# Gating copies on GpSimd, an expert-major normalisation tile and a new front order in an attention and expert-mixture kernel

## The chip, the cores and the metric

The kernel runs on one core of a Trainium2 chip. The metric is the device time of one execution in microseconds (us); a lower time is better. The time before is 957.84 us, the median of three runs (957.78 to 959.23).

A core has five engines with a queue each. PE (TensorE) multiplies matrices, and its rows in the profile are split into matmuls (PE) and weight loads (PEld). DVE (VectorE), ACT (ScalarE) and POOL (GpSimd) work on elements, and SP (SyncE) only issues transfers here. Each engine works through its own queue in order. Transfers are issued from SP's, POOL's and ACT's queues and are carried out by 16 DMA engines.

## The reference

Linear attention on q, k and v (8 batches, 8 heads, 576 tokens, 64 wide) gives an input x of 4608 tokens by 512. Eight experts with 1024 hidden units work on all tokens. The weights P of the experts come from a gate that is normalised over experts and over tokens, eight times in turn.

```python
def phi(x):
    return np.where(x > 0, x, np.exp(x) - 1.0) + 1.0
q_p, k_p = (phi(q), phi(k))
kv = np.einsum('bhsd,bhse->bhde', k_p, v)
z = np.sum(k_p, axis=2)
num = np.einsum('bhsd,bhde->bhse', q_p, kv)
den = np.einsum('bhsd,bhd->bhs', q_p, z)[..., None] + 1e-06
...
logits = x @ w_gate
P = np.exp(logits - logits.max())
for _ in range(8):
    P /= P.sum(1, keepdims=True) + 1e-09
    P /= P.sum(0, keepdims=True) + 1e-09
    P *= N / E
for e in range(E):
    h = np.maximum(x @ w1[e], 0.0)
    out += P[:, e:e + 1] * (h @ w2[e])
```

## The kernel before

**Tiling.** The 4608 tokens are cut into nine groups of 512. SBUF holds x transposed as xT. The expert products are done in two ways. A plain unit runs the full products: `layer1` (L781) and the second layer (L1081). All other units use a Strassen-like scheme with seven products instead of eight, for both layers: `pair` (matmuls at L896) for the first and `layer2` (L1197) for the second. Each needs combinations of its operands: of x (made on DVE at L826 to L831 and stored in DRAM as the blocks xd), of w1 (tile W, L1123), of w2 (tile T, L1137) and of the hidden units (tile S, L1168).

**Stages.** First comes the front, about 110 us: attention batch by batch (`att`), with units of expert 0 between its steps. Behind it come the rest of expert 0 and the normalisation (`sinkhorn`, about 124 to 177 us), and then experts 1 to 7, of which each has nine units of about 12.15 us.

**x blocks.** From expert 1 on the seven blocks of x are read back from DRAM by `x_load` (L873, queue SP) into ten buffers xs0 to xs9 that are reused in turn. The groups form five sub-blocks: (0), (1,2), (3,4), (5,6) and (7,8). The loads of a sub-block are issued as PE frees buffers. The numbers `n` of `l1_half` count half units: n = 0 is sub-block 0, n = 1 and 2 are sub-block 1, n = 3 and 4 sub-block 2, n = 5 and 6 sub-block 3. The list `first_x` collects loads of x, and the weight loads of expert 2 name it as a dependence.

**Weights.** `load_w1` and `load_w2` (issue at L337, queue POOL) fetch the weights of one expert into one of two buffers each. POOL also carries the input loads of the front (L411), two products in each round of the normalisation (L628 and L640), and one accumulation of an output tile in each half unit (L1238), whose operand st ACT has written into one of two staging tiles (L1235).

**Normalisation.** In each of eight rounds POOL multiplies P0 by the row factor Rr (L640) into wt, DVE sums wt over the tokens for each expert into gs (L644), PE sums over the partitions (L649), DVE inverts (L656, L658), POOL multiplies by the column factor cc (L628), and DVE sums over experts and inverts (L635 to L637).

**Order.** `_Plan` is a list scheduler that runs when the program is built. Each task has an engine, a cost, a latency `lat` and a priority. A task of the kind "dma" stands for a transfer; it emits no instruction, and a dependence on it places the dependent task later in the plan but is not by itself a wait on the chip. The waits on the chip follow from the data that an instruction touches. The string `_FRONT` fixes the order of the first tasks by hand (number and engine letter: p PE, a ACT, d DVE, g POOL, s SP, m dma, n none); behind it the scheduler decides. `_FRONT` reaches as far as the last units of sub-block 2 of expert 1.

Of the kernel before, what the change touches and what calls it, by code (L numbers as in the profile page):

```python
# [141 lines left out]
107n 600n 1n 100n 40s 41m 42s 43m 2p 44g 45m 3p 68g 69m 4p 5p 70g 71m 6p 7p 72g 73m 8p 101g  # L142
102m 9p 10p 47d 46a 0g 11p 12p 103g 104m 48d 13p 52n 53a 14p 141g 142m 54d 15p 105g 106m 16p 55d 17p
18p 19p 20p 49n 139g 140m 56p 50p 57d 21p 51a 22p 75d 74a 114g 115m 23p 24p 58p 25p 26p 59a 76d 27p
143g 144m 80p 62a 64p 60p 81n 82n 85d 28p 83a 29p 65d 30p 86a 77n 112g 113m 31p 32p 84d 61a 78p 87d
33p 79a 34p 63a 35p 116g 117m 66p 88p 67d 36p 89a 37p 108g 109m 38p 39p 92a 94p 90p 601p 91a 95d 110g
111m 602p 93a 96p 151p 97d 603p 153n 152n 154a 604p 605p 607p 155d 606a 609p 166g 167m 156d 611p 613p 608d 145a 168g
169m 146d 615p 614a 612d 98g 99m 124p 616d 617p 125n 126n 127a 147d 195g 196m 148n 618a 149p 128d 619p 150d 118a 170g
171m 119d 157p 637n 158a 120d 197g 198m 159p 129d 121n 122p 160a 123d 161a 610d 164p 130p 623p 193g 194m 131a 165d 620d
162p 132p 621p 133a 163d 134a 135p 222g 223m 622p 136d 624p 629a 224g 225m 173d 625p 631a 172a 137p 178p 138d 626p 179n  # L150
180n 181a 249g 250m 174d 638p 226g 227m 182d 640p 633d 627p 639d 175n 183d 205p 176p 641d 206n 207n 208a 628p 253g 254m
177a 209d 280g 281m 642p 199a 200d 184p 643a 644p 201d 278g 279m 185a 210d 646p 202n 228a 645d 186p 203p 647d 187a 648p
204d 188a 229d 211p 191p 305g 306m 658p 212a 192d 307g 308m 635a 230d 213p 189p 214a 650p 190d 231n 649a 234p 651d 232p
235n 236n 251g 252m 237a 256d 652p 282g 283m 255a 238d 656p 670n 233d 215a 220p 653d 332g 333m 239d 309g 310m 216p 221a
217d 240p 659p 241a 257d 242p 666d 218p 243a 657p 258n 219d 284a 285d 261p 259p 262n 263n 264a 359g 360m 671p 260d 336g
337m 673p 265d 672a 244a 266d 675p 674d 664a 267p 247p 677p 268a 248d 676a 286d 269p 245p 270a 679p 246d 287n 678d 290p
288p 680d 292n 291n 293a 681p 312d 311a 294d 660p 295d 271a 661p 388g 389m 289d 363g 364m 274p 296p 275d 683p 297a 361g
362m 313d 682a 272p 317p 339d 314n 654p 318n 319n 320a 273d 685p 338a 321d 315p 556d 298p 392g 393m 316a 655p 340d 563d
299a 322d 334g 335m 668d 276p 684a 300a 704p 277a 323p 301p 686d 302d 706p 365a 324a 390g 391m 303p 703n 662a 705d 325p
304d 326a 327a 415g 416m 689p 344p 346n 345n 347a 366d 564d 341n 342p 343a 367d 395d 348d 690p 697d 708p 330p 331d 371p  # L160
444g 445m 472g 473m 394a 442g 443m 451s 452s 446g 447m 453s 481s 372n 687p 349d 328p 688p 374a 707a 368n 373n 375d 474g
475m 350p 351a 709a 710p 352p 353a 565d 329d 396d 376d 557d 558d 369p 370a 476g 477m 482s 712p 483s 713d 355p 377p 354a
356d 693p 378a 400p 357p 397n 417g 418m 402n 401n 695d 711d 358d 421a 403a 404d 694p 405d 714p 715d 422d 398p 478a 379p
399a 380a 381a 419g 420m 716p 384p 449d 385d 423d 406p 407a 559s 560m 718p 691p 448a 408p 409a 382p 692p 383d 427p 428n
429n 424n 744n 717a 701d 425p 719d 430a 479d 745p 746a 747p 410a 431d 450d 432d 699a 426a 570d 571d 386p 387a 726p 433p
566s 567m 413p 414d 480d 572d 749p 411p 412d 577d 578d 579d 748a 434a 561s 562m 568s 569m 435p 436a 751p 573s 574m 575s
576m 488p 490n 485n 486p 489n 750a 580s 581m 491a 727p 492d 493d 487a 752a 734a 740d 753p 755p 438p 437a 439d 494p 495a
582s 583m 754a 724p 584d 484g 496p 497a 440p 441d 756a 585d 741d 722p 457p 458n 459n 460a 454n 455p 725p 757p 759p 586d
456d 498a 461d 462d 587s 588m 589s 590m 591g 597n 758a 732a 742d 501p 502d 760a 463p 464a 743d 723p 730a 499p 500d 465p
761d 466a 467a 598g 599m 762d 720p 468p 721p 469d 767p 763d 470p 728a 765p 592n 790n 768a 764d 773p 471d 554n 783d 736d  # L170
784d 785d 786s 787m 1014s 1015m 555p 766a 1016s 1017m 503p 771p 504a 505n 506d 737d 507g 791p 772a 792a 769p 805p 788s 789m
738d 1018s 1019m 1020s 1021m 1022s 1023m 508d 739d 841d 795p 796a 775p 1024s 1025m 1026s 1027m 1056s 1057m 1058s 1059m 776d 806a 797p
509p 510d 798a 793p 842d 794a 811p 812a 511g 801p 802d 799p 807p 808a 770a 815p 512d 809p 803p 804a 810a 513g 813p 816d
817p 843d 814d 800d 514d 777p 849p 818a 778a 819d 863p 864a 515p 516d 517g 899d 900d 820d 518d 774d 848n 865p 866a 823p
901d 519g 869p 870a 824a 871p 872d 867p 868a 873p 874d 520d 851p 821d 829p 850a 855p 856a 830a 852a 853p 825p 844s 845m
854a 521p 522d 523g 859p 826d 860d 524d 525g 833p 827p 861p 822d 857p 858d 862a 875p 526d 593g 594m 595g 596m 834d 907p
831p 527p 957d 528d 876a 921p 923p 922a 529g 832d 877d 878d 530d 531g 879d 835p 836a 906n 924a 909p 927p 925p 928a 926a
883p 929p 930d 881p 908a 913p 532d 533p 958d 959d 960s 961m 828a 914a 931p 884d 932d 882a 910a 911p 534d 535g 917p 918d
880d 885p 887p 888a 912a 915p 536d 919p 891p 933p 920a 934a 889p 1060s 1061m 902s 903m 916d 537g 538d 892d 539p 886d 540d
965p 1006d 541g 967p 968a 893p 542d 543g 979p 890d 935d 966a 894a 981p 971p 904s 905m 972a 964n 939p 940a 846s 847m 975p  # L180
973p 969p 970a 982a 936d 976d 544d 1007d 943p 977p 962s 963m 974d 941p 980a 937d 985p 1008d 545p 983p 986a 987p 1009d 978a
989p 546d 984a 1028p 988d 547g 945p 1029a 990d 942a 938d 1030p 991p 548d 1034p 1031a 947p 946d 1035a 549g 992a 1036p 550d 1032p
1037d 1038p 1033a 949p 1039d 551p 1040p 950d 1042p 552d 1044p 1043a 553d 951p 1045a 948d 1041a 1048p 1005n 1062s 1063m 1050p 1046p 1049a
1052p 995p 1070p 1072p 1051d 1064s 1065m 780d 1066s 1067m 1053d 1068s 1069m 1047a 667d 1152s 1153m 944a 1154s 1155m 952a 1073a 663d 1054p
993p 1156s 1157m 1055a 996p 1071a 1126d 1002d 779d 1076p 1127d 1077a 696a 1078p 1074p 1075a 1080p 1518n 999p 1081d 634d 994p 1010d 1011d
1082p 1012d 636d 1084p 1001d 1086p 1085a 1000p 1087a 1090p 1092p 1091a 1088p 632a 997p 1013d 1083a 1094p 1089a 630d 1079d 1093d 1098p 1004a
998p 1099a 1095d 1100p 1096p 1128d 1101a 1129d 1104p 1106p 1003d 1102p 1105a 1130p 1132p 1133d 1097a 1131a 1135p 1134d 1108p 1140p 1109d 1143p
# [52 lines left out]
def kernel(  # L240
# [375 lines left out]
    def sinkhorn():  # L616
# [9 lines left out]
        for it in range(8):  # L626
# [12 lines left out]
            def f_b(_):  # L639
                nc.gpsimd.tensor_tensor(out=wt, in0=P0_sb,  # L640
                                        in1=Rr[:, :, None].broadcast_to([P, NTT, E]), op=ALU.mult)
# [771 lines left out]
```

## Time and profile before

| | |
|---|---|
| median of three runs | 957.84 us |
| the profiled execution | 960.11 us |
| its span (first to last instruction) | 958.3 us |
| mean granted clock of PE | 0.996 |
| idle time of PE in the span | 17.8 us |
| longest sums of waits of PE | on q loads 3.2 us, on x blocks 3.5 us, on the first memset 1.3 us |
| moved by DMA | 112.75 MB, mean 118 GB/s |

A stretch of the profile lists the busy time of each engine in it, the clock that PE was granted and the share of time in which the DMA engines were busy. A row of a timeline gives start, duration, engine, source line, operation, output and input, and in brackets the idle time just before it and what ended that idle time. "us to landing" is the time from the issue of a transfer to its end. Line numbers (L...) are those of the kernel before; in the changed kernel the lines behind L621 stand one further down, and those behind L1004 five.

### The profile page before, as it was taken

To read this page: it belongs to the slowest core of one execution; us is meant where nothing else is said; L and a number is where in the kernel's file an instruction comes from. 1 tells how busy PE (TensorE), PEld (TensorE's weight loads), DVE (VectorE), ACT (ScalarE), POOL (GpSimd) and SP (SyncE) were. 2 spreads that over 40 slices of the span, in tenths; PEclk is the share of its full clock that TensorE was granted. 3 is DMA by queue.
4 is the path that set the end of the run, shared out by engine and by line. 5 is a ranking of instruction groups with operands and counts; after the bars stand their busy time and mean duration, and the time that the engine had idled before them with its cause. 6 is when DMAs were issued, how large, how long until landed. Compare 5 with 4: busy or idle time off the path is not lost.

```text
span 958.3 us, 19980 instructions
## 1 busy us (share of the span) xinstructions
PE 940.5 (98%) x7856; PEld 636.7 (66%) x7856; DVE 772.2 (81%) x1477; ACT 569.8 (59%) x1015; POOL 156.5 (16%) x220
## 2 busy tenths in 40 slices
PE   8999999989999999999999999999999999999997
PEld 3444488656677666766667666766667666776665
DVE  7789999868887888878888888878887888877776
ACT  6789855656655555555555555555555555555551
POOL 6333013011111111111112111111112111111110
PEclk9999999999999999999999999999999999999999
DMA  9989676263226222652226322542226522215554
GB/s 244 261 196 192 198 166 149 77 147 96 78 79 125 78 77 78 152 115 74 66 76 135 101 78 78 129 98 75 72 73 153 120 78 78 72 45 166 165 133 132
DMA packets 82570, 112.75 MB, mean 118 GB/s; under 512 B 7340, under 2 KB 46764, under 8 KB 82476
## 3 DMA queue, kind: packets, MB, share of 16 engines
q1 hardware_dynamic: 56876, 75.59, 26.0%
q0 software_dynamic: 24848, 34.78, 19.4%
q8 instruction: 61, 1.00, 0.4%
q10 hardware_dynamic: 752, 1.11, 0.3%
q14 instruction: 33, 0.27, 0.1%
HBM read 119.69 MB, written 17.69 MB: 143 GB/s over the span
## 4 chain that ended last, share of the span: by engine, by line
PE 80%; DVE 4%; DMA 1%; issue 0%; POOL 0%; DVEq 0%; POOLq 0%
PE ye L1197 34%; PE hq L896 22%; PE R L896 11%; PE Zye L1197 6%; PE Zye L896 6%; DVE hb L930 1%; DMA xs<-xd 1%; DVE xT L1168 1%; PE ye L1081 1%; PE hq L1293 0%; DVE gs L644 0%; PE R L1293 0%; DVE acc L1215 0%; DVE ut L635 0%; DVE acc L1228 0%
## 5 line engine op out<-in xcount | busy, mean ns | idle before, releaser
L1228 DVE SCALAR_TENSOR_TENSOR acc<-ye,P_sb,acc 128x256 f32<-128x256 f32 x620 | 268.1, 479 | 131.7 <-PE ye L1197 129.1
L1197 PEld LDWEIGHTS <-S 128*128 128x128 f16 x1984 | 194.2, 98 | 46.9 <-DVE S L1168 0.2
L1197 PE MATMUL ye<-T,S 128*128 128x256 f16 x1488 | 193.1, 273 | 0.0
L1238 POOL TENSOR_TENSOR acc<-acc,st 128x256 f32<-128x256 f32 x124 | 88.3, 731 | 636.5 <-ACT st L1235 620.9
L1197 PEld LDWEIGHTS <-hb 128*128 128x128 f16 x1584 | 155.3, 98 | 43.7 <-issue 1.7
L896 PEld LDWEIGHTS <-W 128*128 128x128 f16 x1248 | 122.1, 98 | 88.4 <-DMA xs<-xd 2.5
L927 ACT ACTIVATE hb<-hq 128x512 f16<-128x512 f32 x134 | 80.0, 597 | 137.7 <-PE hq L896 134.7
L896 PE MATMUL R<-xs,W 128*128 128x512 f16 (+1 forms) x560 | 150.1, 358 | 2.0 <-DMA xs<-xd 2.0
L896 PE MATMUL hq<-xs,W 128*128 128x512 f16 (+1 forms) x560 | 150.0, 358 | 0.0
L896 PE MATMUL hq<-xs,w 128*128 128x512 f16 (+1 forms) x560 | 139.8, 358 | 0.1
L896 PEld LDWEIGHTS <-w 128*128 128x128 f16 x936 | 91.7, 98 | 61.3 <-issue 2.4
L924 ACT ACTIVATE hb<-Zye 128x512 f16<-128x512 f32 x134 | 80.1, 597 | 38.9 <-PE Zye L896 38.2
L930 DVE CUSTOM_DVE_ANT_0 hb<-hq,sx 128x512 f16<-128x512 f32 x126 | 86.5, 687 | 15.0 <-PE hq L896 14.8
L1235 ACT ACTIVATE st<-Zye,P_sb 128x256 f32<-128x256 f32 x124 | 52.5, 470 | 75.8 <-PE Zye L1197 74.7
L917 ACT COPY sx<-hq 128x512 f32<-128x512 f32 x126 | 73.5, 583 | 37.6 <-PE hq L896 37.5
L913 ACT COPY Zye<-hq 128x512 f32<-128x512 f32 x134 | 77.9, 581 | 23.6 <-PE hq L896 23.4
L930 DVE CUSTOM_DVE_ANT_0 hb<-R,sx 128x512 f16<-128x512 f32 x126 | 86.3, 685 | 5.7 <-ACT sx L917 4.6
L1168 DVE TENSOR_TENSOR S<-hb 128x1024 f16<-128x1024 f16 x124 | 84.9, 685 | 5.9 <-ACT hb L927 5.9
L896 PE MATMUL Zye<-xs,w 128*128 128x512 f16 (+1 forms) x280 | 75.4, 359 | 1.5 <-DMA xs<-xd 1.5
L921 ACT COPY sx<-R 128x512 f32<-128x512 f32 x126 | 74.4, 591 | 1.4 <-PE R L896 1.4
L1197 PE MATMUL ye<-w,hb 128*128 128x256 f16 x528 | 69.3, 275 | 0.5 <-DVE acc L1228 0.5
L1197 PE MATMUL Zye<-w,hb 128*128 128x256 f16 x528 | 68.4, 273 | 0.0
(125 smaller groups left out, 947.1 us busy)
## 6 DMA issues: line engine op xcount, KB each, us to landing
xs<-xd SPq DMA_DIRECT2D x196, 256.0 KB, 3.4
w<-in_moe_w_dram POOLq DMA_DIRECT2D x17, 512.0 KB, 7.9
kin<-in_k_dram POOLq DMA_DIRECT2D x15, 576.0 KB, 7.3
out_dram<-acc SPq DMA_DIRECT2D x61, 128.0 KB, 2.4
w<-in_moe_w_dram POOLq DMA_DIRECT2D x7, 1024.0 KB, 9.9
xs<-xd SPq DMA_DIRECT2D x49, 128.0 KB, 3.3
vv<-in_v_dram POOLq DMA_DIRECT2D x16, 288.0 KB, 7.7
hb<-in_q_dram POOLq DMA_DIRECT2D x15, 288.0 KB, 7.2
```

The costliest lines, as they stand in the source:

```text
L896: nc.tensor.matmul(dst_[:, p, :] if parts == 2 else dst_.rearrange("p a b -> p (a b)"), lhsT=lhs(p, c), rhs=blk[i](c), start=(first and p ...
L913: nc.scalar.copy(out=Zt[1], in_=gX["tile"])
L917: nc.scalar.copy(out=gs2["tile"], in_=gX["tile"])
L921: nc.scalar.copy(out=gs5["tile"], in_=gR["tile"])
L924: nc.scalar.activation(out=dst(0, 0), in_=Zt[1], func=AF.Relu)
L927: nc.scalar.activation(out=dst(1, 0), in_=gX["tile"], func=AF.Relu)
L930: nc.vector._custom_dve(TENSOR_ADD_SAT, out=out_, in0=ps, in1=sb, s0=3.0e38, s1=0.0)
L1168: nc.vector.tensor_tensor(out=Sx[:, i], in0=a0, in1=a1, op=op)
L1197: nc.tensor.matmul(bank(g_)[:, s, :], lhsT=lhs(s, kk), rhs=rhs(kk), start=(new and s == 0 and kk == 0), stop=(kk == 3), skip_group_check=True)
L1228: nc.vector.scalar_tensor_tensor(out=dst(), in0=bank(g_)[:, s, :], scalar=P_sb[:, gg, e:e + 1], in1=dst(), op0=ALU.mult, op1=ALU.add)
L1235: nc.scalar.mul(out=gst["tile"], in_=bank(g_)[:, s, :], mul=P_sb[:, gg, e:e + 1])
L1238: nc.gpsimd.tensor_tensor(out=dst(), in0=dst(), in1=gst["tile"], op=ALU.add)
```

## The change

There are four edits.

1. *Copies.* `first_x` and `second_x` no longer collect the loads of x themselves. At n = 3 and n = 5 a new POOL instruction copies four elements of the last block of the sub-block into the tile `gate`. The loads of expert 2's w1 depend on the first copy, that of w2 on the second.

```diff
         if q == 0:
             st["x"] = x_load(d, un)
-            if n in (1, 3):
-                (first_x if n == 1 else second_x).extend(t for _, t, _ in st["x"].values())
+            if n in (3, 5):
+                gl, tl_, _ = list(st["x"].values())[-1]
+
+                def f_xg(_, gl=gl):
+                    nc.gpsimd.tensor_copy(out=gate, in_=gl["tile"][:, 0, 0, 0:4])
+                (first_x if n == 3 else second_x).append(add(("pool", 0.15), f_xg, deps=[tl_], use=[gl], prio=un - 400.0))
```

2. *Normalisation.* The product by the row factor is written in expert order, so that the sum over tokens reads neighbouring elements.

```diff
+        wc = wt.rearrange("p g e -> p (g e)").rearrange("p (e g) -> p e g", e=E)
...
-                nc.gpsimd.tensor_tensor(out=wt, in0=P0_sb,
+                nc.gpsimd.tensor_tensor(out=wc.rearrange("p e g -> p g e"), in0=P0_sb,
                                         in1=Rr[:, :, None].broadcast_to([P, NTT, E]), op=ALU.mult)
...
-                nc.vector.tensor_reduce(gs, wt.rearrange("p g e -> p e g"), AXX.X, ALU.add)
+                nc.vector.tensor_reduce(gs, wc, AXX.X, ALU.add)
...
-            a = add(("dve", 1.0), f_r, deps=last, prio=-200.0)
+            a = add(("dve", 1.03), f_r, deps=last, prio=-200.0)
             a = add(("pool", 0.9), f_b, deps=[a], prio=-200.0)
-            a = add(("dve", 0.42), f_g, deps=[a], prio=-200.0)
+            a = add(("dve", 0.46), f_g, deps=[a], prio=-200.0)
```

3. *Costs and latencies in the plan.* A w2 load in one piece counts 5.2 us instead of 2.6, and the input loads of attention get a latency of 2.4 instead of 1.95, but for the first two calls of `att`.

```diff
-            ts_.append(add(("dma", costs[len(ts_)] if costs else 2.6), lambda _: None, deps=[ti],
+            ts_.append(add(("dma", costs[len(ts_)] if costs else 5.2 / len(pieces)), lambda _: None, deps=[ti],
...
-            tin[nm] = fadd(("dma", 1.425), lambda _: None, deps=[ti], use=[gr, *gsw], prio=pr, lat=1.95,
+            tin[nm] = fadd(("dma", 1.425), lambda _: None, deps=[ti], use=[gr, *gsw], prio=pr, lat=1.95 if n < 2 else 2.4,
```

4. *The order.* `_FRONT` is replaced as a whole.

```diff
-107n 600n 1n 100n 40s 41m 42s 43m 2p 44g 45m 3p 68g 69m 4p 5p 70g 71m 6p 7p 72g 73m 8p 101g
...
+1n 600n 100n 107n 40s 41m 42s 43m 2p 3p 0g 4p 44g 45m 5p 6p 68g 69m 7p 8p 70g 71m 9p 72g
...
```

What this moves in the built programs:

- POOL builds the identity (task 0g) before the first input load instead of after the fifth transfer. The third k load of POOL's queue stands ahead of the third q load; before, it stood two loads behind it.
- PE has 24 first-layer matmuls in a row ahead of the transposes (L484) of that third q load; before, it had 20.
- Expert 1's w1 goes out in two steps, after the first and after the fourth round's first product, and w2 after the sixth; before, w2 went first of all and both halves of w1 after the fourth. DVE's combinations of w1 begin after the fifth round instead of after the sixth.
- Of expert 2's weights, w1 now stands behind the first copy and one accumulation, and w2 behind the second copy. Before, w2 and both halves of w1 stood together behind the first accumulation of expert 1.
- From about 195 us of the span of before on, where expert 1's second layer begins with its seven products, the order of PE's matmuls is the same in both programs.

More of the change, by code (lines that the diff above doesn't have):

```diff
@@ L147 @@
[L147 to L151, printed above, removed]
@@ new lines @@
+64p 34p 65d 35p 116g 117m 63a 36p 88p 66p 89a 37p 67d 38p 39p 92a 108g 109m 90p 94p 601p 91a 95d 110g
+111m 602p 93a 151p 96p 153n 152n 603p 154a 97d 604p 605p 155d 607p 606a 609p 156d 168g 169m 611p 613p 608d 166g 167m
+146d 615p 614a 145a 617p 119d 195g 196m 616d 118a 147d 124p 193g 194m 619p 126n 125n 120d 127a 148n 170g 171m 149p 637n
+612a 128d 150a 620d 157p 121n 98g 99m 122p 158a 129d 123a 610d 159p 164p 160a 618d 161a 130p 222g 223m 621p 131a 623p
+165d 162p 132p 163d 133a 622p 197g 198m 134a 624p 629d 137p 226g 227m 631d 178p 625p 179n 180n 181a 138d 627p 173d 172a
@@ new lines @@
+182d 628p 174d 249g 250m 135p 635a 205p 136d 224g 225m 626p 206n 207n 208a 200d 251g 252m 638p 183d 640p 209d 175n 199a
+639d 176p 201d 278g 279m 642p 177a 228a 641d 282g 283m 184p 229d 644p 185a 202n 210d 643a 186p 203p 187a 646p 204d 253g
+254m 188a 645d 305g 306m 191p 211p 648p 212a 192d 647a 230d 189p 213p 656p 214a 190d 231n 649a 256d 234p 232p 236n 235n
+633d 237a 650p 309g 310m 233d 255a 238d 652p 285d 215a 220p 332g 333m 670n 239d 280g 281m 653d 218p 221a 240p 219d 658p
+241a 651d 284a 261p 257d 216p 262n 659p 263n 264a 217d 359g 360m 258n 657p 307g 308m 265d 259p 664a 266d 242p 671p 243a
@@ new lines @@
+260d 286d 244a 267p 247p 660p 268a 248d 661p 311a 666d 269p 312d 245p 673p 270a 287n 246d 290p 674a 672d 288p 292n 291n
+293a 313d 675p 336g 337m 271a 388g 389m 294d 677p 334g 335m 295d 289a 654p 338a 676d 363g 364m 296p 274p 361g 362m 297a
+679p 275d 678a 272p 680d 298p 314n 655p 299a 273d 339d 317p 315p 319n 318n 320a 415g 416m 681p 316d 390g 391m 300a 321d
+683p 322d 682a 276p 668a 340d 685p 366d 277a 684a 556d 303p 703n 323p 704p 324a 304d 563d 344p 705a 301p 345n 444g 445m
+686d 689p 347a 341n 346n 302d 392g 393m 706p 662a 348d 365a 342p 564d 557d 325p 446g 447m 343a 690p 558d 326a 349d 442g
@@ new lines @@
+443m 708p 327a 707d 367d 328p 350p 710p 329d 351a 394a 709d 330p 352p 368n 395d 687p 353a 331d 472g 473m 712p 354a 711d
+371p 396d 369p 372n 373n 474g 475m 374a 697d 451s 714p 476g 477m 452s 421a 453s 375d 693p 370d 713a 400p 355p 401n 417g
+418m 688p 403a 356d 481s 376d 357p 695a 716p 402n 397n 404d 715a 482s 358d 377p 694p 378a 405d 717a 483s 379p 398p 559s
+560m 380a 718p 399d 419g 420m 381a 565d 484g 566s 567m 384p 406p 561s 562m 691p 407a 385d 701a 422d 408p 382p 409a 692p
+383d 568s 569m 410a 719d 427p 744n 413p 423d 428n 429n 745p 430a 414d 747p 746a 431d 478a 424n 425p 570d 386p 479d 426a
@@ new lines @@
+448a 432d 749p 571d 387a 748a 577d 411p 433p 726p 434a 572d 412d 573s 574m 750a 435p 575s 576m 578d 751p 436a 480d 699a
+449d 488p 485n 486p 489n 490n 491a 579d 724p 450d 580s 581m 487a 582s 583m 492d 725p 437a 727p 732a 493d 440p 734a 740d
+494p 753p 495a 441d 752a 741d 496p 438p 497a 720p 454n 439d 498a 742d 457p 499p 743d 459n 458n 721p 460a 500d 755p 754a
+461d 728a 455p 756a 757p 456a 462d 584d 501p 463p 759p 464a 502d 758a 465p 760d 468p 466a 722p 761d 467a 723p 585d 762d
+765p 730a 469d 790n 586d 470p 767p 471d 587s 588m 763d 554n 555p 783d 503p 766a 784d 769p 785d 504a 768a 736d 505n 786s
@@ new lines @@
+543g 941p 972a 939p 979p 964n 970a 980a 975p 976d 981p 940a 982a 973p 544d 974d 985p 945p 987p 943p 986a 977p 946a 978a
+988d 545p 546d 983p 984a 989p 547g 990d 1028p 1030p 1029a 949p 548d 549g 938d 1034p 991p 942a 1031a 947p 1036p 1032p 550d 950d
+948d 1035a 1038p 1039d 951p 551p 1040p 1033a 552d 553d 1037d 1005n 992a 952a 1042p 1043a 993p 994p 1044p 1048p 1041a 696a 1045a 665a
+995p 1049a 1050p 1046p 897a 1052p 1070p 1062s 1063m 1001a 1064s 1065m 1072p 1010d 1047a 1071a 996p 1073a 1011d 1012d 700d 1053d 1054p 1076p
@@ L236 @@
+2143a 2140p 2218d 2298s 2146p 2141a 2299m 2145d 2190p 2300s 2192p 2147d 2191a 2301m 2173p 2219d 2193a 2148p 2220d 2196p 2174d 2149a 2302s 2198p
+2175d 2197a 2303m 2194p 2221d 2222p 2195a 2199d 2224p 2223a 2227p 2225d 2226d 2200p 2228a 2232p 2230a 2201d 2229g 2235p 2231g 2233d 2234d 2202p
+2236d
 """
```

149 lines of the change are left out of this document (61 added, 88 removed).

## The prediction

> **What bounds the kernel now.** I read the page first, then the stretches, then what PE waited for.
>
> ```profile
> span 958.3 us, 19980 instructions
> PE 940.5 (98%) x7856; PEld 636.7 (66%) x7856; DVE 772.2 (81%) x1477; ACT 569.8 (59%) x1015; POOL 156.5 (16%) x220
> PE 80%; DVE 4%; DMA 1%; issue 0%; POOL 0%; DVEq 0%; POOLq 0%
> ```
>
> TensorE (PE) is busy for 940.5 of 958.3 us, and 80% of the chain that ended last is PE work. Both programs send PE the same number of instructions (15690 rows each when the orders are laid side by side, the 38 filler matmuls among them). So the change can move the time only through the 17.8 us in which PE idles and the stretches in which its clock is reduced. In the stretches of the span:
>
> ```profile
> 200.00:220.00 20.00, 16.55 (x101) 10.34 (x100) 13.98 (x29) 10.47 (x20) 3.44 (x5) 0.91 0.91 197
> 300.00:400.00 100.00, 100.00 (x710) 69.17 (x708) 80.58 (x157) 56.31 (x106) 15.06 (x21) 1.00 0.35 91
> ```
>
> The columns are length, then busy time of PE, weight load, DVE, ACT and POOL, then PEclk, DMA share and GB/s. From 300 us on nothing is to be had before the tail: PE is busy for 100 of 100 us at full clock. In 200 to 220 it idles 3.45 us, and the granted clock is 0.91. The timeline of PE shows where:
>
> ```profile
> 201.97 0.59 PE L896 MATMUL R<-xs,W 128*128 128x512 f16 x2
> ...
> 208.00 0.61 PE L896 MATMUL R<-xs,W 128*128 128x512 f16 x2 [1.97 <-DMA xs<-xd]
> 210.08 1.01 PE L896 MATMUL Zye<-xs,w 128*128 128x512 f16 x2 [1.48 <-DMA xs<-xd]
> ...
> 231.57 0.59 PE L896 MATMUL R<-xs,W 128*128 128x512 f16 x2
> ```
>
> Two matmul pairs of expert 1 wait for x blocks (tile xs) of sub-block 2 that are still under way. Two finer stretches give the clock's share, and two early ones will be needed below:
>
> ```profile
> 25.00:30.00 5.00, 3.45 (x66) 1.54 (x59) 4.69 (x8) 4.30 (x6) 1.69 (x3) 0.89 1.24 207
> 30.00:35.00 5.00, 5.00 (x28) 1.64 (x27) 2.56 (x5) 2.85 (x4) 1.92 (x3) 0.77 1.29 262
> ...
> 206.00:211.00 5.00, 1.55 (x6) 0.58 (x6) 2.67 (x5) 0.60 (x2) 0.00 (x0) 0.88 1.12 270
> 211.00:216.00 5.00, 5.00 (x36) 3.87 (x35) 2.03 (x5) 2.66 (x5) 0.52 (x1) 0.78 1.10 263
> ```
>
> The loss in clock is 5 x 0.12 + 5 x 0.22 = 1.7 us. The stall costs 1.97 + 1.48 + 1.7 = 5.15 us.
>
> **Why the blocks are late.** POOL's timeline and the transfers:
>
> ```profile
> 198.74 2.43 POOL L337 DMA_DIRECT2D w<-in_moe_w_dram  x3
> ...
> 215.48 2.27 POOL L1238 TENSOR_TENSOR acc<-acc,st 128x256 f32<-128x256 f32 x3 [14.31 <-ACT st L1235]
> 227.63 0.81 POOL L1238 TENSOR_TENSOR acc<-acc,st 128x256 f32<-128x256 f32 x1 [9.88 <-ACT st L1235]
> 232.81 0.72 POOL L1238 TENSOR_TENSOR acc<-acc,st 128x256 f32<-128x256 f32 x1 [4.38 <-DVE acc L1228]
> 239.78 0.95 POOL L1238 TENSOR_TENSOR acc<-acc,st 128x256 f32<-128x256 f32 x1 [6.25 <-ACT st L1235]
> ```
>
> ```profile
> xs<-xd SPq DMA_DIRECT2D x196, 256.0 KB, 3.4
> w<-in_moe_w_dram POOLq DMA_DIRECT2D x17, 512.0 KB, 7.9
> w<-in_moe_w_dram POOLq DMA_DIRECT2D x7, 1024.0 KB, 9.9
> ...
> xs<-xd SPq DMA_DIRECT2D x10, 256.0 KB, 11.7
> w<-in_moe_w_dram POOLq DMA_DIRECT2D x2, 512.0 KB, 17.1
> ```
>
> All three loads of expert 2's weights leave POOL from 198.74 on, just when SP sends the x blocks whose buffers PE frees about 200. A block lands in 3.4 us over the whole run, and in 11.7 us in the stretch from 180 to 230. The DMA engines are full there (share 1.12 and 1.10). In the program of before nothing holds the weights back behind the blocks.
>
> **The change part by part.**
>
> *The copies (-5.15).* In the changed program w1 of expert 2 stands behind a POOL copy that reads the last x block of sub-block 2 and waits for its transfer; one accumulation on POOL stands between. The load of w2 stands behind a copy that reads the last block of sub-block 3. So the blocks of sub-block 2 have the engines to themselves. The buffer of the block that stalled first comes free about 1.5 us before the pair at 201.97 (the pairs run through the blocks in one order), and 200.5 + 3.4 lands two microseconds ahead of its need at 206.03 (208.00 - 1.97). I take the whole 5.15 off. The bounds are 0 and 5.15.
>
> What is paid: two copies, each like this one, on an engine that is busy for 16% of the span.
>
> ```profile
> L445 POOL CAST gate<-vv x1: 292/292/292, 95.0 to 95.0; 128x4 f32<-128x4 f16 x1
> ```
>
> Behind the first copy wait one accumulation and w1. Its block is freed by the pair at 201.97 and lands about 206.3; the accumulation after it could not run before 215.48 - 5.15 = 210.3 anyway. So w1 leaves at 211.1, and its second half 0.75 us later, landing near 220 by the 7.9 us row. DVE needs it next:
>
> ```profile
> 154.85 0.20 DVE L658 RECIPROCAL cc<-Dc 128x8 f32<-128x8 f32 x1
> 160.49 0.65 DVE L1123 TENSOR_TENSOR W<-w 128x1024 f16<-128x1024 f16 x1
> ...
> 229.55 0.68 DVE L1123 TENSOR_TENSOR W<-w 128x1024 f16<-128x1024 f16 x1
> 258.40 0.94 DVE L1137 TENSOR_TENSOR T<-w 128x1024 f16<-128x1024 f16 x1
> ```
>
> The weight combination keeps its place in DVE's order, so it comes at 229.55 - 5.15 = 224.4, four microseconds after w1. If that cover went, DVE would stop with all evictions behind it. The second copy waits for a block that the pair at 231.57 - 5.15 = 226.4 frees; it lands near 230.5. POOL stands from 223.3 until then. Behind it queue w2 (leaves at 231, lands at 241, needed at 253) and the accumulation that ran at 232.81, now at 231.7 instead of 227.7. ACT has two staging tiles: the next one (accumulated at 239.78 - 5.15 = 234.6) is free already. ACT would be held only if the copy lasted until about 239. Cost: nothing.
>
> *The front's order (-1.7).* With the latency of later loads entered as 2.4 instead of 1.95, PE meets its loads 0.45 us later relative to their issue. Four waits in the attention part are of this kind:
>
> ```profile
> 56.90 0.48 PE L484 MATMUL att<-ident,hb 64*64 64x64 f16 x36 [0.82 <-DMA hb<-in_q_dram]
> ...
> 78.48 0.48 PE L484 MATMUL att<-ident,hb 64*64 64x64 f16 x36 [1.30 <-DMA hb<-in_q_dram]
> 96.39 0.48 PE L484 MATMUL att<-ident,hb 64*64 64x64 f16 x36 [0.35 <-DMA hb<-in_q_dram]
> 97.97 0.70 PE L454 MATMUL kv_ps<-vv,t 64*64 64x128 f16 x36 [1.10 <-DMA vv<-in_v_dram]
> ```
>
> 0.45 + 0.45 + 0.35 + 0.45 = 1.7 us off; at most all 3.57. The loss bound is another wait of the same kind at each place, +3.6. In the first 40 us four more matmuls stand ahead of the transposes of POOL's third q load, but a k load is now ahead of that q in POOL's queue, and the identity is built before the first load. These pull both ways: I take 0, between -3.25 (25 to 35 us: 1.55 us of idle and 0.55 + 1.15 of clock) and +3.25, the same loss once more.
>
> *Normalisation (0).* The scaled terms are written in expert order, and the sum over tokens then reads contiguously.
>
> ```profile
> L644 DVE TENSOR_REDUCE gs<-wt x8: 656/668/675, 126.5 to 173.2; 128x8 f32<-128x288 f32 x8
> L640 POOL TENSOR_TENSOR wt<-P_sb,Rr x8: 682/685/936, 125.1 to 172.5; 128x288 f32<-128x288 f32 x8
> L635 DVE TENSOR_REDUCE ut<-wt x7: 439/446/453, 130.4 to 171.2; 128x36 f32<-128x288 f32 x7
> ```
>
> ```profile
> PE R L649 <- DVE gs L644: 0.9, 2, 0.4
> ```
>
> The reduce should go from 0.668 to the 0.446 of its contiguous sister, 8 x 0.22 = 1.8 us of DVE; PE waited 0.9 us for it in all, and that is the most to gain. No row has a POOL write with a stride. I bound it between nothing and the slowest row of the same line, 0.936, so +0.25 x 8 = 2.0 us, against the 1.8 won: 0, from -0.9 to +0.2.
>
> [...]
>
> *Sum.* -5.15 - 1.7 + 0 + 0 = -6.85 us. The profiled execution took 960.11 us, 1.8 around its span; it becomes 953.3. The median of the runs, 2.27 below it, becomes 957.84 - 6.85 = **951.0 us**.
>
> **The rivals.**
>
> (a) *The front gives everything:* all 3.57 and 3.25 go, and the gs waits too: 957.84 - 5.15 - 3.57 - 3.25 - 0.9 = 945.0; half of that beyond the forecast is about 948. For it: all these are load waits. Against: DMA share 1.24 and 1.29 says that early loads wait for bandwidth, which no order makes.
>
> (b) *Part of the stall stays,* since the late blocks still share the engines with earlier ones: 1.48 us without loss of clock, 952.5. [...]
>
> (c) *The copies do not hold the weights,* or the blocks are late for another cause: only the front's 1.7 comes, 956.1. Against: the copy waits for the transfer's semaphore in the built program.
>
> (d) *Slower: expert 1's w1 comes too late.* Its second half still leaves after the fourth scaling,
>
> ```profile
> 145.40 1.48 POOL L337 DMA_DIRECT2D w<-in_moe_w_dram  x2
> ```
>
> ```profile
> w<-in_moe_w_dram POOLq DMA_DIRECT2D x1, 512.0 KB, 5.4
> ```
>
> ```profile
> 150.00:155.00 5.00, 4.58 (x42) 3.89 (x41) 4.86 (x13) 3.22 (x7) 0.94 (x1) 1.00 0.71 143
> ```
>
> but DVE's combination is now one iteration earlier, behind the cc at 154.85 instead of at 160.49. It has 9.6 us instead of 15. At 17.1, the slow row of its kind, DVE stops 7.5 us, and there, busy for 4.86 of 5 us, it can absorb nothing: evictions, scaling and the buffers that open after normalisation all follow. With one loss of clock and a repeat at the x blocks behind it (1.7 + 1.97): 951.0 + 7.5 + 3.7 = 962. It decides from a landing of 9.6 us, and makes the kernel slower from about 13. Against: 5.4 us at this place.
>
> (e) *The front loses at every place:* 957.84 - 5.15 + 3.6 + 3.25 = 959.5, or about 957.5 at two thirds.
>
> **How the numbers follow.** Forecast with (b): 0.68, own range 948.5 to 954.5. (a) 0.12, (c) 0.05, (d) 0.07, (e) 0.08. The range is 946.5 to 957.0: it cuts off (d), most of (e) and the far end of (a). A measurement of this kernel tells 0.2%, 1.9 us, from no change. Faster (below 955.9): forecast and (b), (a), and half of (c), 0.83; within 0.2%: 0.06; slower: (d) and part of (e), 0.11.
>
> **What would show it.** Right: no idle of PE on xs between 195 and 225 us, PEclk 1.00 there, blocks landing in under 5 us, the weight loads of expert 2 in two groups about 211 and 231, POOL idle at both copies without ACT behind it, the gs reduce near 0.45 us, the four load waits together under 2.5 us. Wrong: a new wait of DVE on w1, of PE on gs or on loads before 120 us, or a dip of PEclk at a new place.

## The result, and the profile after

The changed kernel takes 951.68 us (median of four runs, 951.31 to 953.62) against 957.81 us (four runs) for the kernel before: 6.13 us less, a ratio of 0.9938 with a 95% interval from 0.9921 to 0.9955. The forecast was 951.0. The profiled execution took 953.62 us, 6.49 less than the one before the change.

From the page of the changed kernel, its span, the busy time of the engines and the chain that ended last:

```profile
span 951.8 us, 19990 instructions
PE 939.6 (99%) x7856; PEld 636.5 (67%) x7856; DVE 766.0 (80%) x1467; ACT 575.8 (60%) x1025; POOL 157.4 (17%) x222
PE 90%; DVE 5%; DMA 3%; issue 1%; ACT 0%; POOL 0%; DVEq 0%; POOLq 0%
```

PE idles 12.2 us instead of 17.8. Where that came from shows in three stretches (length, busy time of PE, weight load, DVE, ACT and POOL, PEclk, DMA share, GB/s), of the kernel before:

```profile
0.00:120.00 120.00, 111.65 (x1846) 52.20 (x1846) 101.10 (x163) 95.06 (x126) 40.52 (x61) 0.99 0.95 218
120.00:185.00 65.00, 63.94 (x582) 53.47 (x581) 59.98 (x129) 38.59 (x72) 13.48 (x17) 1.00 0.57 145
185.00:260.00 75.00, 71.55 (x463) 45.68 (x461) 60.17 (x116) 46.27 (x87) 9.99 (x13) 0.98 0.38 95
```

and of the changed one, with the stretch of the old stall below:

```profile
0.00:120.00 120.00, 114.69 (x1872) 54.19 (x1873) 100.20 (x162) 97.28 (x130) 38.89 (x59) 0.99 0.94 212
120.00:185.00 65.00, 63.90 (x572) 53.26 (x570) 55.56 (x123) 43.13 (x80) 15.24 (x19) 1.00 0.64 156
185.00:260.00 75.00, 74.40 (x502) 48.70 (x500) 66.39 (x126) 49.83 (x95) 12.41 (x17) 1.00 0.42 102
200.00:220.00 20.00, 20.00 (x141) 13.55 (x139) 17.15 (x35) 13.51 (x26) 3.29 (x6) 1.00 0.55 132
```

Idle time of PE falls from 8.35 to 5.31 us in the front, stays at 1.06 and 1.10 in the normalisation, and falls from 3.45 to 0.60 behind it. The stall at 206 us is gone, its loss of clock too. The chain is now 90% PE.

The blocks of the changed kernel between 180 and 230 us, the stretch in which they took 11.7 us before, and POOL's timeline there (start, duration, instruction, and in brackets the idle time before and what ended it):

```profile
xs<-xd SPq DMA_DIRECT2D x15, 256.0 KB, 4.1
```

```profile
203.71 0.19 POOL L1010 CAST gate<-xs 128x4 f32<-128x4 f16 x1 [6.60 <-DMA xs<-xd]
207.65 0.73 POOL L1243 TENSOR_TENSOR acc<-acc,st 128x256 f32<-128x256 f32 x1 [3.76 <-ACT st L1240]
208.32 1.48 POOL L337 DMA_DIRECT2D w<-in_moe_w_dram  x2
...
219.80 0.81 POOL L1243 TENSOR_TENSOR acc<-acc,st 128x256 f32<-128x256 f32 x1 [9.24 <-ACT st L1240]
228.56 0.33 POOL L1010 CAST gate<-xs 128x4 f32<-128x4 f16 x1 [7.95 <-DMA xs<-xd]
229.02 0.92 POOL L337 DMA_DIRECT2D w<-in_moe_w_dram  x1
```

Blocks land in 4.1 us instead of 11.7, and expert 2's weights leave in two groups. But read the brackets: copy 1 is done at 203.9, and POOL then waits 3.76 us for ACT before the accumulation that stands ahead of w1. So w1 is held by the accumulation. Only w2 is held by its copy, from about 220.6 to 229.02. This is a reading of one trace; the experiments below test it.

PE's waits in the changed kernel (sum, times, longest), and the normalisation's two changed lines:

```profile
PE att L484 <- DMA hb<-in_q_dram: 1.2, 1, 1.2
PE R L650 <- DVE gs L645: 1.1, 3, 0.7
PE kv_ps L454 <- DMA vv<-in_v_dram: 0.8, 1, 0.8
...
PE hq L897 <- DVE hb L931: 0.4, 1, 0.4
```

```profile
L645 DVE TENSOR_REDUCE gs<-wt x8: 434/442/452, 125.6 to 170.6; 128x8 f32<-128x288 f32 x8
```

```profile
L641 POOL TENSOR_TENSOR wt<-P_sb,Rr x8: 692/722/968, 124.2 to 169.6; 128x288 f32<-128x288 f32 x8
```

The sum over tokens went from 0.668 to 0.442 us, and POOL's write with a step costs 0.722 instead of 0.685 (medians). Nevertheless PE waits 1.1 us for gs, where it waited 0.9 before.

### The profile page after: what moved, and what is told of

Read it like the earlier page. It is cut to its first block, busy times and chain, and to the rows that moved or that the text cites. A ratio compares the mean times of both kernels' runs of the same rounds, so it can differ in the third digit from the quotient of the medians.

```text
span 951.8 us, 19990 instructions
## 1 busy us (share of the span) xinstructions
PE 939.6 (99%) x7856; PEld 636.5 (67%) x7856; DVE 766.0 (80%) x1467; ACT 575.8 (60%) x1025; POOL 157.4 (17%) x222
## 3 DMA queue, kind: packets, MB, share of 16 engines
q10 hardware_dynamic: 752, 1.11, 0.4%
## 4 chain that ended last, share of the span: by engine, by line
PE 90%; DVE 5%; DMA 3%; issue 1%; ACT 0%; POOL 0%; DVEq 0%; POOLq 0%
PE ye L1202 35%; PE hq L897 23%; PE R L897 12%; PE Zye L1202 6%; PE Zye L897 6%; PE ye L1086 3%; PE hq L782 2%; DMA w<-in_moe_w_dram 1%; DMA hb<-in_q_dram 1%; DVE xT L1173 1%; DMA vv<-in_v_dram 1%; PE kv_ps L454 1%; PE att L553 0%; PE num_ps L553 0%; PE att L484 0%
```

## The experiments

The kernels ran in three groups, each on one chip beside the kernel before: e1 to e4; c0, e5, e6 and e7; c1, e4b, e8 and e9 (c0 and c1 are the changed kernel itself). Each was timed five to twelve times. Kernels of one group are compared by their medians; over groups, by the ratio to the kernel before. The ranges in brackets go from the fastest to the slowest execution.

### The copies and the place of the weight loads

**e7_first_copy_gone, e6_order_alone and c0_after (one group).** In e7 a memset takes the place of copy 1 alone. In e6 both copies are memsets, and w2 moves behind the next accumulation in POOL's queue.

```diff
 # e7
-                    nc.gpsimd.tensor_copy(out=gate, in_=gl["tile"][:, 0, 0, 0:4])
+                    if n == 3:
+                        nc.gpsimd.memset(gate, 0.0)
+                    else:
+                        nc.gpsimd.tensor_copy(out=gate, in_=gl["tile"][:, 0, 0, 0:4])
 # e6
-                    nc.gpsimd.tensor_copy(out=gate, in_=gl["tile"][:, 0, 0, 0:4])
+                    nc.gpsimd.memset(gate, 0.0)
-1530d 1239p 1287s 1288m 1289g 1525n 1526g 1527m 1259a ... 1399m 1260g 1290p
+1530d 1239p 1287s 1288m 1289g 1259a ... 1399m 1260g 1525n 1526g 1527m 1290p
```

> The changed kernel itself, as it is, beside the other runs of this call: 951.7, between 951 and 953.6. It is the measure that the others are held against. If the theory of the clock in the front holds (about 1.7 us of clock at 30 to 34 us come or go from one execution to the next at nearly the same idle time), its runs differ by about that much, with mean granted clocks between 0.997 and 1.000.

> The changed kernel with a memset in place of the first copy alone; the second one stays. Theory (w1 is held by the accumulation behind the first copy, so that copy holds nothing): w1 leaves near 206 to 208 us as with it, no wait on xs between 195 and 235 us, 951.7. Rival (the first copy carries part of the gain): PE waits on xs near 203 to 208 us, 953 to 955. If both the theory here and the loss without both copies hold, the second copy alone carries the gain of the copies.

> The changed kernel with memsets in place of both copies (no wait for x blocks) and the w2 load one accumulation later in POOL's queue. Theory (what counts is that w2's transfer does not share the engines with the blocks of sub-block 3; any place that is late enough does it): w2 leaves at 223 to 226 us instead of 218 without the copy and 229 with it, the last blocks of sub-block 3 are on their way already, PE waits on xs for less than 0.5 us near 227: 951.7 to 952.5. Rival (five microseconds are not enough, only the wait for the last block is): PE waits 1 us or more on xs there, 953 to 954.7.

Measured: c0 950.96 us (950.17 to 952.04), e7 951.13 (950.53 to 951.25), e6 950.48 (950.11 to 952.05). One row of POOL's timeline each, e7 and then e6:

```profile
206.28 1.48 POOL L337 DMA_DIRECT2D w<-in_moe_w_dram  x2
```

```profile
223.25 0.91 POOL L337 DMA_DIRECT2D w<-in_moe_w_dram  x1
```

Without copy 1, w1 leaves at 206.28 us; with it, in c0, at 205.78. Copy 1 holds nothing. Without copy 2 but one accumulation later, w2 leaves at 223.25, while the blocks of sub-block 3 are still on their way; neither PE nor its clock loses anything on xs (20.00 of 20 us busy at a clock of 1.00 from 220 to 240 us). Both theories are confirmed: a place in the queue that is late enough suffices. By medians e6 can't be told apart from the changed kernel; in its trace PE doesn't have the changed kernel's wait of 0.42 us for an eviction, which comes back under the hardware below.

**e1_no_wait.** Both copies become memsets, and the order stays.

```diff
-                    nc.gpsimd.tensor_copy(out=gate, in_=gl["tile"][:, 0, 0, 0:4])
+                    nc.gpsimd.memset(gate, 0.0)
```

> The changed kernel with both copies replaced by a memset of the same tile at the same place of POOL's queue: nothing waits for an x block any more, the order of all engines stays. Theory (w1 is held by the accumulation behind the first copy, which waited for ACT until 207.65 us, and the second copy holds w2 alone): w1 still leaves near 208 us, w2 leaves near 220.6 us instead of 229, and its 1 MB shares the DMA engines with the blocks of sub-block 3; PE loses 0 to 2.6 us (half of the old stall, at a later place): 951.7 to 954. Rival (the waits of the copies carry the whole gain): all of the 5.15 us comes back, 956.8, with PE idle on xs near 206 us. Rival (the waits are worth nothing, the place in the queue does everything): 951.7.

Measured: 954.66 us (953.67 to 956.11), ratio 0.9953 [0.9935, 0.9971]. PE's timeline, POOL's, and two fine stretches of e1:

```profile
227.09 0.60 PE L897 MATMUL R<-xs,W 128*128 128x512 f16 x2 [1.80 <-DMA xs<-xd]
228.49 1.01 PE L897 MATMUL Zye<-xs,w 128*128 128x512 f16 x2 [0.80 <-DMA xs<-xd]
```

```profile
205.80 1.48 POOL L337 DMA_DIRECT2D w<-in_moe_w_dram  x2
...
218.08 0.91 POOL L337 DMA_DIRECT2D w<-in_moe_w_dram  x1
```

```profile
228.00:230.00 2.00, 1.51 (x6) 0.75 (x6) 0.00 (x0) 0.00 (x0) 0.00 (x0) 0.63 1.05 360
230.00:232.00 2.00, 2.00 (x11) 1.40 (x10) 0.00 (x0) 0.57 (x1) 0.00 (x0) 0.52 0.56 214
```

The mechanism was forecast rightly, the size too low: w1 still leaves at 205.80 and does no harm, w2 leaves at 218.08 and a stall comes back at sub-block 3, with 2.60 us of idle, the upper end of the forecast, and 2 x 0.37 + 2 x 0.48 = 1.7 us of clock, which the forecast left out. The median lies above the forecast's 954. The stall is read from the trace; by time alone e1 and the changed kernel, of two groups, are not clearly apart, since the intervals of their ratios overlap. With e6, whose w2 leaves 5 us later without a wait for the blocks, copy 2 matters only because without it w2 would leave too early at this place of the queue.

**e2_weights_early and e8_weights_earlier_still.** The weights of expert 2 lose their dependence on the copies and stand together in the old place, behind the second (e2) or the first accumulation (e8) of expert 1.

```diff
-... load_w1(e, prio=float(e), deps=w_t[e - 1][1][1:] + (first_x if e == 2 else [])) + load_w2(e, ..., deps=w_t[e - 1][3][1:] + (second_x if e == 2 else []))
+... load_w1(e, prio=float(e), deps=w_t[e - 1][1][1:] + []) + load_w2(e, ..., deps=w_t[e - 1][3][1:] + [])
-1139g 669a 1121d 1137g 1151d
+1139g 669a 1121d 1137g 1525n 1526g 1527m 1520n 1521g 1522m 1523g 1524m 1151d    # e2
+1139g 1525n 1526g 1527m 1520n 1521g 1522m 1523g 1524m 669a 1121d 1137g 1151d    # e8
```

> The changed kernel, but expert 2's weight loads no longer depend on the copies and stand together behind the second accumulation of expert 1 in POOL's queue, as before the change; the copies stay and hold nothing. Theory (the weights beside the blocks made the stall): PE waits for xs near 206 us again, blocks land in about 12 us there, +5.15 us: 956.8. Rival (the blocks were late because of the old front order, not because of the weights): no wait on xs, 951.7 to 952. Rival (part of the stall stayed anyway): less than 5.15 comes back, 953.5 to 955.

> The changed kernel with expert 2's loads again without the copies' hold, and one accumulation (0.75 us) earlier still in POOL's queue than in the run with 953.2. Theory (the head start of the weights over the blocks sets how late the blocks land: 0.83 us of head start gave blocks of 9.0 us and one wait of 1.72 us, 1.69 us in the program of before gave 11.7 us and 3.45 us of waits in two, and the clock): blocks land in 11 to 12 us, PE waits on xs for 2.5 to 3.5 us near 203 us and loses 1.7 us of clock besides: 955 to 956.5. Rival (the old front itself made the blocks later, by its order of the buffers): 1.7 us of waits as in that run, no loss of clock, 953.

Measured: e2 953.23 us (952.59 to 955.01), 0.9940 of the kernel before, where the changed kernel has 0.9938, so that the price of e2's wait is seen in the trace alone; e8 956.26 (953.17 to 957.40), 4.55 above the changed kernel in the same group (c1 below). PE's timelines, e2 and then e8:

```profile
203.36 0.59 PE L897 MATMUL Zye<-xs,w 128*128 128x512 f16 x2 [1.72 <-DMA xs<-xd]
```

```profile
202.79 0.61 PE L897 MATMUL R<-xs,W 128*128 128x512 f16 x2 [2.01 <-DMA xs<-xd]
204.41 0.59 PE L897 MATMUL Zye<-xs,w 128*128 128x512 f16 x2 [1.01 <-DMA xs<-xd]
```

And the transfers of the blocks between 193 and 216 us, e2 and e8:

```profile
xs<-xd SPq DMA_DIRECT2D x7, 256.0 KB, 9.0
```

```profile
xs<-xd SPq DMA_DIRECT2D x7, 256.0 KB, 11.1
```

The start of the weight loads on POOL and of the blocks on SP, e2 and then e8:

```profile
194.67 2.34 POOL L337 DMA_DIRECT2D w<-in_moe_w_dram  x3
195.50 5.52 SPq L874 DMA_DIRECT2D xs<-xd  x7
```

```profile
193.49 2.34 POOL L337 DMA_DIRECT2D w<-in_moe_w_dram  x3
195.18 5.52 SPq L874 DMA_DIRECT2D xs<-xd  x7
```

By itself e2 spoke for the rival that only part of the stall hangs on the weights. Then e8 settled it: from the first load of the weights to the first block, e2 gives them 195.50 - 194.67 = 0.83 us of head start, e8 195.18 - 193.49 = 1.69, and the kernel before had 200.43 - 198.74 = 1.69. The blocks then land in 9.0, 11.1 and 11.7 us, and PE idles 1.72, 3.02 and 3.45 us. With the new front and the new layout in place, the place of the loads alone brings the old stall back.

### The front order and the normalisation

**e3_old_front_weights_late.** The kernel before, without copies, with only the weight loads of expert 2 moved in its order string: w1 to its place after the change, w2 behind the next accumulation, one place later than in the changed kernel and the same as in e6.

```diff
-1080p 1518n 999p ... 1200p 1523n 1196d 1524g 1525m 1199a ... 1519g 1520m 1202d 1201d 1521g 1522m ... 1205g 1211p ... 1259g 1288p
+1080p 999p ... 1200p 1196d 1199a ... 1202d 1201d ... 1205g 1518n 1519g 1520m 1521g 1522m 1211p ... 1259g 1523n 1524g 1525m 1288p
```

> The kernel before the change, with its own front order and normalisation, without copies; only expert 2's w1 and w2 are moved in POOL's queue to the two places that they have after the change. Theory (the place of the loads is what brings the 5.15 us): 957.8 - 5.15 = 952.7, PE without idle time on xs between 195 and 225 us, and the four load waits of the attention part at their old 3.57 us. Rival (without the copies' waits the loads come early enough to delay the blocks): 955 to 957.8. The difference to the changed kernel is what front order and normalisation bring: 1.0 by this theory (2.7 of waits won, some of it lost again in the first 40 us).

Measured: 953.13 us (952.14 to 953.62), 5.10 below the 958.23 of the kernel before in the same group; the forecast of the move was 5.15. No wait on xs between 195 and 225 us. w2 leaves at 226.65 us; the changed kernel's place for it, without a copy, is what e1 tested.

**e4_old_normalisation, and e4b_old_normalisation beside c1_after.** The old layout of the scaled terms in the changed kernel; e4b is the same kernel, run beside the changed one.

```diff
-                nc.gpsimd.tensor_tensor(out=wc.rearrange("p e g -> p g e"), in0=P0_sb,
+                nc.gpsimd.tensor_tensor(out=wt, in0=P0_sb,
-                nc.vector.tensor_reduce(gs, wc, AXX.X, ALU.add)
+                nc.vector.tensor_reduce(gs, wt.rearrange("p g e -> p e g"), AXX.X, ALU.add)
```

> The changed kernel with the old layout of the scaled terms: POOL writes in order, DVE sums with a step. Theory (DVE's saved time is covered; only PE's waits for gs count): the sum goes back from 0.44 to 0.67 us eight times, 1.8 us of DVE, and the time rises by 0 to 0.9 us: 951.7 to 952.6. Rival (every 0.22 us of DVE counts, since DVE has no idle time to spare in the normalisation): +1.8 us, 953.5. Rival (POOL's write with a step costs more than it saves): -0.3 to -1 us, 951.

> The changed kernel itself, as it is, as the measure for the other runs of this call: 951.0 to 951.7.

> The changed kernel with the old layout of the scaled terms, now beside the changed kernel itself. Theory (only what PE waits for gs counts, 2.2 us with the old layout and 1.1 with the new one in the profiles so far): +1.1 us, 952.1 to 952.8. Rival (all of the 1.8 us of DVE counts): +1.8. Rival (the forecast's own value): 0.

Measured: e4 953.89 us (951.58 to 954.56) in the group of e3; c1 951.71 (951.27 to 952.34) and e4b 952.04 (951.72 to 952.45) in one group. PE's waits between 120 and 185 us in e4b; c1's row is that of the changed kernel above, 1.1 us:

```profile
PE R L650 <- DVE gs L645: 2.2, 3, 1.1
```

The new layout takes 1.1 us of waits from PE, of which the medians show 0.33 us; the ranges of the two overlap, so this difference is not clear of noise. The rival that all 1.8 us of DVE count falls. e4 spread over 3 us and said little; e4b replaced it.

**e9_old_front_new_normalisation.** e3 with the new layout, beside c1: all of the change but the front order and the copies, with w2 at the place that it has in e3 and e6.

```diff
+        wc = wt.rearrange("p g e -> p (g e)").rearrange("p (e g) -> p e g", e=E)
-                nc.gpsimd.tensor_tensor(out=wt, in0=P0_sb,
+                nc.gpsimd.tensor_tensor(out=wc.rearrange("p e g -> p g e"), in0=P0_sb,
-                nc.vector.tensor_reduce(gs, wt.rearrange("p g e -> p e g"), AXX.X, ALU.add)
+                nc.vector.tensor_reduce(gs, wc, AXX.X, ALU.add)
```

> The kernel before the change with the weight loads at their late places, by order alone, and with the new layout of the scaled terms: all of the change but the new front order and the copies. Theory (front order: 2.7 us of load waits won, up to 0.9 of it given back in the first 40 us): 1 to 2.7 us above the changed kernel, 952 to 954.4. Rival (the front brings nothing, since what a load wait loses, the next wait gains): equal to the changed kernel. Rival (the new layout gains nothing at the old front, where PE's waits for gs were 0.9 us in all): the same as the run of the old front with the old layout, 953.1.

Measured: 951.43 us (951.07 to 954.72) against c1's 951.71. By medians the old front is not slower. The other pair of one group, both with the old layout, says the same: e3 with the old front 953.13, e4 with the new one 953.89. By means the first pair turns round: e9 has four executions from 951.07 to 951.60 and two at 954.55 and 954.72, the profiled one, so its mean is 0.63 us above c1's, while e3's is 0.55 below e4's. No pair shows a gain near 1.7. The stretches and the wait for gs, e9:

```profile
0.00:120.00 120.00, 112.28 (x1837) 51.99 (x1838) 99.57 (x161) 94.01 (x125) 39.86 (x61) 0.97 0.94 218
120.00:185.00 65.00, 64.72 (x593) 54.39 (x592) 59.98 (x131) 39.67 (x74) 14.28 (x18) 1.00 0.58 143
185.00:260.00 75.00, 74.92 (x506) 49.20 (x505) 65.56 (x126) 49.86 (x93) 11.05 (x15) 1.00 0.43 104
```

```profile
PE R L650 <- DVE gs L645: 0.2, 1, 0.2
```

and c1's stretches:

```profile
0.00:120.00 120.00, 113.92 (x1907) 55.37 (x1908) 101.98 (x166) 97.98 (x132) 39.21 (x59) 1.00 0.94 215
120.00:185.00 65.00, 63.89 (x541) 52.33 (x540) 55.60 (x122) 43.89 (x80) 15.28 (x19) 1.00 0.63 151
185.00:260.00 75.00, 74.50 (x506) 49.18 (x505) 65.24 (x125) 49.55 (x94) 12.61 (x17) 1.00 0.42 102
```

The new front idles 6.08 us to 120 us, the old one 7.72: 1.64 won. In the normalisation it is 1.11 against 0.28: 0.83 given back, because PE waits 1.1 us for gs instead of 0.2. Behind it, 0.50 against 0.08: 0.42 given back. What is left, 0.4 us, is less than these medians can tell. e3 and e4 leave the same 0.4 us by the same three stretches. The last 0.42 us belong to copy 2 and the place of w2: e6, with the new front but without the copies, idles 0.08 there.

**e5_q_before_k.** One pair of the new front put back: the third q load of POOL's queue ahead of the third k load.

```diff
-57d 22p 51a 112g 113m 75d 23p ... 77n 143g 144m 84d
+57d 22p 51a 75d 23p ... 77n 143g 144m 112g 113m 84d
```

> The changed kernel with the third k load of POOL's queue moved behind the third q load, as before the change. Theory (the k that went ahead delays the q that PE waits for at 24 us): the wait of 0.7 to 1.2 us on that q goes or halves, and with less idle time the clock loss at 30 to 34 us comes more seldom: -0.5 to -2, 950 to 951. Rival (the early loads wait for bandwidth, which no order makes): k is late by what q wins, PE waits elsewhere before 40 us, 951.7. Rival (the k load is the more urgent one, as the new order has it): +0.5 to +2, 952.2 to 953.7.

Measured: 953.53 us (951.95 to 955.39), 2.57 above c0 of the same group. DVE's and PE's timelines of e5:

```profile
24.92 0.76 DVE L429 TENSOR_SCALAR t<-kin 128x1152 f16<-128x1152 f32 x1 [2.94 <-DMA kin<-in_k_dram]
25.60 0.68 DVE L789 TENSOR_SCALAR hb<-hq 128x512 f16<-128x512 f32 x1
```

```profile
26.33 1.02 PE L782 MATMUL hq<-xT,w 128*128 128x512 f16 x4 [2.45 <-DVE hb L789]
```

PE doesn't wait on the third q, but neither does it in c0's profile, so that the theory of a q delayed by the k ahead of it isn't shown. DVE now stands 2.94 us at the late k, an eviction (hb) stands behind it, and PE waits 2.45 us for that. The rival that k is the more urgent load was right. c0 has neither wait.

## Why the prediction was right, and where it was not

The total is right: -6.13 for -6.85. Its parts are not all, and that the total came so near is partly luck: the place of the loads (5.10 us, e3), the layout (0.33) and the front with the copies (0.28 to 0.76 lost) sum to 4.7 to 5.2 us by medians, and the 1.0 to 1.5 us that are left are assigned to no part.

*The stall (-5.15): right in cause and size, wrong in one link.* The place of the loads is worth 4.55 us (e8 to c1) to 5.10 (kernel before to e3). The prediction credited the first copy with holding w1, though its own working had the accumulation behind it as the later of the two. w1 is held by the accumulation, and the copy could go (e7). The second copy does hold w2 and is needed at this place of the queue (e1), though one place later would do (e6). The forecast times were near: w1 at 211.1, in fact 208.32; w2 at 231, in fact 229.02; neither was late for DVE.

*The copies' price (0): nearly right.* It is a wait of PE of 0.42 us in the trace; what the traces show beside it stands under the hardware.

*Rival (b), part of the stall stays:* not in the changed kernel, which has no wait on xs; e2 shows what it would be. That such a rest costs no clock was the rival's assumption: e2's wait of 1.72 us cost none in any of six executions (mean clocks 0.999 and 1.000), e1's two waits of 1.80 and 0.80 us came with a loss of 1.7 us of clock.

*The front order (-1.7): not found in the times; the step left out what follows.* "PE meets its loads 0.45 us later" held, and more: of the four load waits of 3.57 us only 0.85 is left. In the first 40 us the sum of 0 held in the profiled executions (4.58 us of idle before, 4.16 after, 1.7 of clock lost in both). e5 tests one of the two pulls there, and it has the other sign: the prediction counted the k load ahead of q against the new order, but putting it back costs 2.57 us, near the bound of 3.25. Above all the step took a wait that is gone for time that is won: under the new front PE waits 1.1 us for gs, under the old one, with the same layout, 0.2.

By idle time part of the gain stays. Up to 185 us PE idles 5.4 to 7.2 us in the eight profiled executions with the new front and the new layout (the changed kernel, c0, c1, e1, e2, e6, e7, e8), and 8.0 in the one with the old front (e9); c1, the one compared above, is the highest of the eight. By time the two pairs of one group show nothing. With the stall in both programs front and layout together bring 957.69 - 956.26 = 1.43 us (kernel before to e8). Whether the front is worth 1.7 us or less, these runs don't settle.

Where gs is later can be read in DVE's timeline, though no run tests it. In c1's round with the longest wait (0.7 us) five other instructions stand between the row factor, done at 135.16, and the sum at 138.25: 3.09 us, and DVE is busy throughout. In e9's rounds at 132 and 139 us it is four, and 2.2 us.

*The normalisation (0, from -0.9 to +0.2): within its bounds.* -0.33 us by medians, not clear of noise. POOL's write was bounded at +0.25 a time and costs +0.037 (0.722 against 0.685).

*The other rivals:* (a) fell, since the front brought nothing like 10 us; (c) was true of copy 1 alone, and it didn't matter; (d) fell, since DVE combined expert 1's w1 without a stop; (e) fell as a whole, though e9 shows its kind of give-back in small.

## What to carry to other kernels

When a transfer that PE needs at once and a prefetch share the DMA engines, put the prefetch late enough behind the urgent transfers; here that was worth 4.55 us (e8 to c1), and a later place in its queue did it as well as a wait (e6 950.48 us, c0 950.96). The wait also moved what stands behind it in the queue: the accumulation behind copy 2 starts at 227.25 us in c0 and at 222.59 in e6. Before crediting a wait to the instruction that the change names, read in the queue's timeline which instruction ended last. A load wait taken from the bounding engine counts only after it is seen that the next stage doesn't wait longer for it; here PE's wait for gs was 1.1 us under the new front and 0.2 under the old (c1, e9).

## What the runs showed of the hardware

**The granted clock was lost in steps of 1.7 to 1.8 us.** The stall of before, e1's and the front's loss of the changed kernel (0.54 and 0.61 from 30 to 34 us) each cost 1.7 us, as did the front's loss in the kernel before (0.72, 0.50 and 0.93 from 28 to 34 us), but not in each execution: from 20 to 40 us c1 idles 2.56 us at a clock of 1.00, the changed kernel 2.66 at 0.91. e9's profiled execution has two such steps, 1.8 us from 20 to 40 us (20 x 0.09, with 0.50 and 0.71 from 30 to 34) and 1.8 from 80 to 120 us (20 x 0.05 + 20 x 0.04), and takes 3.3 us more than e9's median. With the loads late, the mean clock is 0.998 or less in 5 of 12 executions with the old front (e3, e9) and in 5 of 38 with the new one (the changed kernel, c0, c1, e4, e4b, e6, e7); whether the order does this was not tested. e8's profiled execution has two waits of 3.02 us in sum and keeps its clock:

```profile
200.00:220.00 20.00, 16.98 (x118) 11.34 (x117) 14.55 (x28) 10.75 (x21) 1.58 (x3) 1.00 0.66 160
```

It took 953.72 us at a mean clock of 0.999. Ten of the twelve executions of e8 have 0.996 to 0.998 and take 955.4 to 957.4; that they lost it at this stall is inferred from the steps. The sum of the idle time doesn't decide it alone: e1 lost the clock with 1.80 and 0.80 us of idle and a matmul pair between, e8's profiled execution kept it with 2.01 and 1.01 us, also with a pair between. The 3.45 us of the old stall, which lost it, are two waits with a pair between as well (1.97 and 1.48). What decides it the traces don't show.

**Two DVE instructions of c0 took longer beside POOL's accumulations than they did in e6.** DVE's and POOL's timeline in c0, and the same in e6:

```profile
226.96 1.59 DVE L1173 TENSOR_TENSOR S<-hb 128x1024 f16<-128x1024 f16 x1
...
229.25 0.68 DVE L1173 TENSOR_TENSOR S<-hb,S 128x1024 f16<-128x1024 f16 x1
229.85 0.95 DVE L1071 TENSOR_SCALAR acc<-acc,P_sb 128x512 f32<-128x512 f32 x1
```

```profile
227.25 0.74 POOL L1243 TENSOR_TENSOR acc<-acc,st 128x256 f32<-128x256 f32 x1
229.42 1.09 POOL L1243 TENSOR_TENSOR acc<-acc,st 128x256 f32<-128x256 f32 x1 [1.44 <-ACT st L1240]
```

```profile
227.09 0.69 DVE L1173 TENSOR_TENSOR S<-hb 128x1024 f16<-128x1024 f16 x1
...
229.44 0.48 DVE L1071 TENSOR_SCALAR acc<-acc,P_sb 128x512 f32<-128x512 f32 x1
```

```profile
229.57 0.94 POOL L1243 TENSOR_TENSOR acc<-acc,st 128x256 f32<-128x256 f32 x1 [5.41 <-ACT st L1240]
```

In c0 the first and the last of these DVE instructions run beside POOL's accumulations and take 0.90 and 0.47 us longer than in e6; both end 0.3 to 0.6 us after the accumulation. Not every overlap cost time: the instruction at 229.25 starts 0.17 us before the second accumulation and takes its usual 0.68, and in e6 L1071 starts 0.13 us before one and takes 0.48. What decides this the traces don't show. In c0 PE then waits 0.42 us for an eviction; in e6 it doesn't. That the two engines hinder each other is not shown: no run here takes the POOL instruction away alone.
